# Fewer, larger transfers in a fused cross-attention and SwiGLU kernel: 220 transfers for 312

## The chip, the cores and the metric

The kernel runs on one core of a Trainium2 chip. The core has a matrix engine (TensorE, PE in the profile; the loading of its weights is listed apart as PEld), a vector engine (VectorE, DVE), an engine for activation functions and copies (ScalarE, ACT), a general one (GpSimd, POOL), and SyncE (SP), which issues transfers only. Transfers between the off-chip memory (DRAM) and the on-chip memory are issued from two queues here, SyncE's and ScalarE's, and are carried by 16 transfer engines. The metric is the time of one execution in microseconds on the device; the kernel before takes 755.71 us (median of 3 runs, 754.4 to 756.5).

## The reference

Eight batches with eight heads each; x has 512 tokens of 64 features per head, the state 32 rows per head. Cross attention runs both ways: tokens read the state, and state rows read the tokens. The results, 544 rows of 512 features per batch, then go through a normalisation and a gated feed-forward block.

```python
def _attn_ref(x, state):            # x (8, 8, 512, 64), state (8, 8, 32, 64)
    scores = scale * np.matmul(x, state.transpose(0, 1, 3, 2))
    ...
    xread = np.matmul(a, state)     # a = softmax of scores, over the state's rows
    scores2 = scale * np.matmul(state, x.transpose(0, 1, 3, 2))
    ...
    sread = np.matmul(a2, x)        # a2 = softmax of scores2, over the tokens
    return np.concatenate([xread, sread], axis=2)

def _moe_ref(x, w_gate, w_val, w_out, rms_g):   # x (4352, 512), w_gate (512, 1536)
    rms = np.sqrt(np.mean(x * x, axis=-1, keepdims=True) + 1e-06)
    xn = x / rms * rms_g
    g = xn @ w_gate
    silu = g * (1.0 / (1.0 + np.exp(-g)))
    return (silu * (xn @ w_val)) @ w_out
```

## The kernel before

The 512 tokens of a batch are worked on as one stage, batch after batch; the state rows of all batches together (256 rows) come last. For each batch TensorE multiplies the batch's state into the gate and value weights (`own_weights`, L703), runs the hidden layer as seven block products instead of eight (`hidden_seven`, L850), and the output projection as seven times seven quarter products (`project_twice`, L1153). The state rows go through `hidden_seven` and `project_seven` (L1016).

The order of all instructions is written out by hand. Each piece of work is a generator, a stream named by a letter, which yields after every step; strings of letters (ORDER, FIRST, PERIOD, LAST, STATES) say which stream takes its next step. Each engine runs its instructions, and issues its transfers, in exactly that order. While batch b is in its hidden layer and projection, the streams `a` (`tokens_read`) and `s` (`states_read`) prepare batch b + 1.

For batches 2 to 7, x has to be turned so that features lie on partitions. `scores` does that without TensorE: VectorE transposes blocks of 32 by 32 (L340) into `xB`, ScalarE's queue writes it to a scratch in DRAM (`x_d`, 1024 KB, L342) and reads it back with the blocks in another order (`xG`, four transfers of 256 KB, L347). A wait for the write stands in front of the first read, on ScalarE's queue. TensorE multiplies the result with the state (L357). In `states_read` the exponentials go the same way: transposed into `eB`, written to `e_d` (512 KB, L629), read back into `e2` (four transfers of 128 KB, L633), and multiplied with x (L644). Other instructions of ScalarE, such as the copies of the products out of TensorE's banks (L715, L897 to L904), stand in the same queue, between these issues.

In `project_twice`, ScalarE copies the partial products to a tile `kept` (L1163), VectorE adds more of them (L1193), GpSimd forms the four quarters from seven products in `combine` (L1179 to L1184), and `stores` sends two blocks of 128 rows by 256 columns through `store_tokens` (L1261) on SyncE's queue. `store_states` (L1268) writes the final state rows, one transfer per batch. `load_state` (L130) loads a batch's state with four transfers. Beside these SyncE fetches prepared weights (`w_m<-w_d`, L197, 1024 KB; `w<-t_d`, L1099, 576 KB).

## Time and profile before

| what | us |
| --- | --- |
| median of 3 runs (lowest, highest) | 755.71 (754.4, 756.5) |
| the profiled execution: time | 758.14 |
| the profiled execution: span | 756.4 |
| TensorE busy | 748.6 |
| VectorE, ScalarE, GpSimd busy | 580.0, 352.6, 296.3 |
| SyncE's transfers, share of the 16 engines' time | 46.4% |
| ScalarE's transfers, share of the 16 engines' time | 8.7% |
| granted TensorE clock, mean | 0.997 |

The profile comes from one execution. Its span runs from the first to the last instruction; the time of that execution also has what lies around the span. Each line of the profile names the line of the kernel, the engine and the operation, and the tiles as output<-input. A line of an engine with a q, such as ACTq or SPq, is the issue of a transfer by that engine's queue; the transfer itself lands later. In brackets stands how long an engine was idle before an instruction and what released it. Busy time of TensorE is modelled at its ends, so a busy TensorE is not one at its peak.

### The profile page before, as it was taken

To read this page: it belongs to the slowest core of one execution; us is meant where nothing else is said; L and a number is where in the kernel's file an instruction comes from. 1 tells how busy PE (TensorE), PEld (TensorE's weight loads), DVE (VectorE), ACT (ScalarE), POOL (GpSimd) and SP (SyncE) were. 2 spreads that over 40 slices of the span, in tenths; PEclk is the share of its full clock that TensorE was granted. 3 is DMA by queue.
4 is the path that set the end of the run, shared out by engine and by line. 5 is a ranking of instruction groups with operands and counts; after the bars stand their busy time and mean duration, and the time that the engine had idled before them with its cause. 6 is when DMAs were issued, how large, how long until landed. Compare 5 with 4: busy or idle time off the path is not lost.

```text
span 756.4 us, 14396 instructions
## 1 busy us (share of the span) xinstructions
PE 748.6 (99%) x5636; PEld 600.4 (79%) x5636; DVE 580.0 (77%) x982; ACT 352.6 (47%) x549; POOL 296.3 (39%) x387
## 2 busy tenths in 40 slices
PE   9999999999999999999999999999999999999998
PEld 7734344769978898879877997799788987899997
DVE  3989876569957996689848994799579965787962
ACT  4999892445245623644255425543456236411220
POOL 3100016961484227532465129312842275323600
PEclk9999999999999999999999999999999999999999
DMA  9787935861777186725673467517661865132411
GB/s 293 245 292 267 381 145 196 294 236 36 281 233 244 27 305 203 272 56 212 238 275 112 168 240 251 178 66 303 215 224 27 305 205 217 53 99 112 140 56 29
DMA packets 61891, 146.17 MB, mean 193 GB/s; under 512 B 15744, under 2 KB 32640, under 8 KB 54912
## 3 DMA queue, kind: packets, MB, share of 16 engines
q1 hardware_dynamic: 48704, 125.78, 46.4%
q10 hardware_dynamic: 13120, 19.47, 8.7%
q8 instruction: 45, 0.74, 0.4%
q14 instruction: 22, 0.18, 0.1%
HBM read 116.46 MB, written 28.77 MB: 192 GB/s over the span
## 4 chain that ended last, share of the span: by engine, by line
PE 94%; DVE 2%; POOL 2%; DMA 1%; issue 0%; ACT 0%; POOLq 0%
PE f L850 38%; PE f L1153 29%; PE f L953 6%; PE pv L746 6%; PE at L703 3%; PE pv L703 2%; PE f L1285 2%; PE f L1016 2%; DMA xG<-x_d 1%; PE at L357 1%; PE at L644 1%; PE at L450 1%; PE pv L517 0%; POOL w L1107 0%; PE at L308 0%
## 5 line engine op out<-in xcount | busy, mean ns | idle before, releaser
L850 PE MATMUL f<-aT_s,v 128*128 128x256 f32 x504 | 120.6, 384 | 0.0
L850 PEld LDWEIGHTS f<-aT_s,v 128*128 128x128 f32 x504 | 95.0, 191 | 24.4 <-issue 10.2
L1179 POOL TENSOR_TENSOR kept<-kept 128x256 f32<-128x256 f32 x28 | 23.1, 825 | 191.9 <-DVE kept L1193 190.7
L913 DVE TENSOR_TENSOR g<-g,f 128x512 f32<-128x512 f32 x84 | 57.4, 686 | 40.6 <-PE f L850 35.3
L1163 ACT COPY kept<-f 128x512 f32<-128x512 f32 (+1 forms) x56 | 29.7, 533 | 125.3 <-PE f L1153 83.4
L850 PE MATMUL f<-aT_t,vs 128*128 128x256 f32 x336 | 87.8, 385 | 0.2 <-POOL vs L730 0.2
L850 PEld LDWEIGHTS f<-aT_t,vs 128*128 128x128 f32 x336 | 63.2, 192 | 15.7 <-POOL vs L730 3.9
L1153 PE MATMUL f<-w,h 128*128 128x128 f32 x588 | 74.6, 276 | 0.0
L1153 PEld LDWEIGHTS f<-w,h 128*128 128x128 f32 x588 | 69.7, 192 | 4.9 <-issue 4.9
L904 ACT ACTIVATE hb<-g 128x1024 f32<-128x1024 f32 x42 | 44.4, 1058 | 54.9 <-DVE g L913 54.8
L730 POOL TENSOR_TENSOR vs<-v 128x256 f32<-128x256 f32 x42 | 31.7, 756 | 85.2 <-ACT v L715 85.2
L301 POOL TENSOR_TENSOR ri<-ss,mhalf 128x4 f32<-128x4 f32 (+1 forms) x9 | 12.5, 1385 | 98.9 <-DVE ss L382 67.6
L902 ACT COPY g<-f 128x512 f32<-128x512 f32 x42 | 24.6, 586 | 44.9 <-PE f L850 44.9
L953 PE MATMUL f<-wo,hb 128*128 128x512 f32 x96 | 44.9, 600 | 0.0
L746 PE MATMUL pv<-aT_s,v 128*128 128x512 f32 x96 | 44.1, 595 | 0.0
L850 PE MATMUL f<-aT_s,vs 128*128 128x256 f32 x168 | 43.6, 382 | 0.0
L926 DVE TENSOR_TENSOR hb<-hb,f 128x512 f32<-128x512 f32 (+1 forms) x48 | 31.1, 647 | 16.3 <-PE f L850 16.3
L850 PE MATMUL f<-aT_t,v 128*128 128x256 f32 x168 | 43.5, 381 | 0.0
L926 DVE TENSOR_TENSOR hb<-hb,c 128x512 f32<-128x512 f32 (+1 forms) x48 | 37.9, 789 | 6.6 <-ACT hb L904 5.9
L1153 PE MATMUL f<-wo,h 128*128 128x128 f32 x336 | 42.2, 275 | 0.0
L1153 PE MATMUL f<-wo,hb 128*128 128x128 f32 x336 | 42.1, 275 | 0.0
L913 DVE TENSOR_TENSOR c<-c,f 128x512 f32<-128x512 f32 (+1 forms) x48 | 31.3, 651 | 12.5 <-PE f L850 12.5
(225 smaller groups left out, 1678.2 us busy)
## 6 DMA issues: line engine op xcount, KB each, us to landing
w_m<-w_d SPq DMA_DIRECT2D x48, 1024.0 KB, 5.9
w<-t_d SPq DMA_DIRECT2D x49, 576.0 KB, 5.4
out_dram<-kept SPq DMA_DIRECT2D x56, 128.0 KB, 1.9
raw<-in_moe_w_val_dram SPq DMA_DIRECT2D x6, 1024.0 KB, 5.5
raw<-in_moe_w_out_dram SPq DMA_DIRECT2D x6, 1024.0 KB, 8.2
w_d<-w_m SPq DMA_DIRECT2D x6, 1024.0 KB, 4.9
x_b<-in_x_dram SPq DMA_DIRECT2D x6, 1024.0 KB, 7.4
x_d<-xB ACTq DMA_DIRECT2D x6, 1024.0 KB, 4.2
```

Of the source, the lines that this page charges most:

```text
L703: TE.matmul(out=pv[e][Ns * j:Ns * j + Ns, :], lhsT=stT_g[b][D * e:D * e + D, j, :], rhs=w[D * e:D * e + D, j].rearrange("p m k f -> p (m k ...
L730: GE.tensor_tensor(out=vs[:, 0], in0=a21, in1=a22, op=ALU.add)
L746: TE.matmul(out=to[0], lhsT=lhs(i, k), rhs=r, start=(i == 0), stop=(i == len(rhs) - 1))
L850: TE.matmul(out=ps[:, i, 0:half], lhsT=l[:, i, :], rhs=r, start=(start and i == 0 and k == 0), stop=(k == len(lhs) - 1), skip_group_check= ...
L902: SE.copy(gates(q)[1], q["x"][:, :, 0:half])
L904: SE.activation(out=hb[:, 2 * mp:2 * mp + 2, 0:n].rearrange("p m (c t) -> p m c t", c=2), in_=q["g"][:, :, :, 0:half], func=ACTF.Silu if s ...
L913: VE.tensor_tensor(out=to, in0=to, in1=q[ps][:, :, 0:half], op=ALU.add)
L926: VE.tensor_tensor(out=part, in0=part, in1=val, op=ALU.mult)
L953: TE.matmul(out=banks[r], lhsT=hb[:, m, P * r:P * r + P], rhs=wo[:, m, :], start=(m == 0), stop=(m == NM - 1))
L1153: TE.matmul(out=to[half][:, slot, :], lhsT=lhs[:, k, :], rhs=rhs[:, k, :], start=(fresh and n in (0, 4) and k == 0), stop=(k == QM - 1), s ...
L1163: SE.copy(k[:, 4 * i:4 * i + 4 - i], banks[name][i])
L1179: GE.tensor_tensor(out=k[:, 1:3], in0=k[:, 0:1].to_broadcast([P, 2, QD]), in1=k[:, 1:3], op=ALU.add)
```

## The change

Six kinds of transfer are merged; the number of transfers issued goes from 312 to 220. The scratch of x changes its layout so that a single transfer can write it (a partition's 2048 values as one run) and a single one can read it; the same holds for the exponentials. Where the reads were four steps of their stream, the one read is followed by empty steps (`yield from range(4)`), so that the strings of letters still fit. The token stores take 256 rows at once; for that the seven products lie in other slots of their banks and `combine` writes the quarters in the order in which they are stored. The final state rows of four batches go in one transfer, and the state rows of a batch come in two transfers instead of four.

```diff
     def load_state(b):
         rows[b] = two.tile([P, 2, D], F32, name="rows")
-        for j in range(4):
-            src = state[b, 2 * j:2 * j + 2].rearrange("e n d -> n e d")
-            nc.sync.dma_start(out=rows[b][Ns * j:Ns * j + Ns], in_=src)
+        for e in range(2):
+            nc.sync.dma_start(out=rows[b][:, e], in_=state[b, e::2])
...
-    x_d = [scratch.tile([4, 4, Ns, 4 * P], F32, name="x_d%d" % k) for k in range(2)]
-    e_d = [scratch.tile([4, Ns, 4, 8 * Ns], F32, name="e_d%d" % k) for k in range(2)]
+    x_d = [scratch.tile([Ns, 4, 4, 4 * P], F32, name="x_d%d" % k) for k in range(2)]
+    e_d = [scratch.tile([Ns, 4, 4, 8 * Ns], F32, name="e_d%d" % k) for k in range(2)]
...
-            nc.scalar.dma_start(out=x_d[b % 2].rearrange("q g f r -> (g f) q r"),
-                                in_=xB.rearrange("p q j c t -> p q (j c t)"))
+            nc.scalar.dma_start(out=x_d[b % 2].rearrange("f g q r -> g f (q r)"),
+                                in_=xB.rearrange("p q j c t -> p (q j c t)"))
             yield
             xT = one.tile([P, 4, 4, P], F32, name="xG", tag="xT")
-            for q in range(4):
-                nc.scalar.dma_start(
-                    out=xT[Ns * q:Ns * q + Ns].rearrange("f g j r -> f g (j r)"),
-                    in_=x_d[b % 2][q].rearrange("g f r -> f g r"))
-                yield
+            nc.scalar.dma_start(out=xT.rearrange("p g j r -> p g (j r)"),
+                                in_=x_d[b % 2].rearrange("f g q r -> q (f g) r"))
+            yield from range(4)
...
-            nc.scalar.dma_start(out=e_d[b % 2].rearrange("j t g f -> (j t) (g f)"),
+            nc.scalar.dma_start(out=e_d[b % 2].rearrange("t j g f -> j t (g f)"),
                                 in_=eB.rearrange("p g e c n -> p (g e c n)"))
             yield
-            for g in range(4):
-                nc.scalar.dma_start(out=e2T[Ns * g:Ns * g + Ns].rearrange("t j e c n -> t j (e c n)"),
-                                    in_=e_d[b % 2][:, :, g].rearrange("j t f -> t j f"))
-                yield
+            nc.scalar.dma_start(out=e2T.rearrange("p j e c n -> p j (e c n)"),
+                                in_=e_d[b % 2].rearrange("t j g f -> g (t j) f"))
+            yield from range(4)
...
-                        (0, 0, a11, b11), (0, 2, a12, b21), (0, 3, a22, 2), (0, 1, 1, 1),
-                        (1, 2, 0, 0), (1, 1, 2, b12), (1, 0, 3, b22))):
+                        (0, 1, a11, b11), (0, 0, a12, b21), (0, 2, a22, 2), (0, 3, 1, 1),
+                        (1, 0, 0, 0), (1, 1, 2, b12), (1, 2, 3, b22))):
...
+        def of_half(k, i):
+            return k[:, 1:4] if i else k[:, 4:8]
...
         def stores():
             for what in ("p1", "p5", "u2", "c21"):
-                for r in range(2):
-                    store(*ready[what][r])
-                    yield
+                store(*ready[what])
+                yield
+                yield

         def combine(what, i, j):
             k = kept[what]
-            ready[what] = []
-            GE.tensor_tensor(out=k[:, 1:3], in0=k[:, 0:1].to_broadcast([P, 2, QD]), in1=k[:, 1:3],
+            GE.tensor_tensor(out=k[:, 4:8:3], in0=k[:, 5:6].to_broadcast([P, 2, QD]), in1=k[:, 4:8:3],
                              op=ALU.add)
-            GE.tensor_tensor(out=k[:, 5:8:2], in0=k[:, 1:2].to_broadcast([P, 2, QD]),
-                             in1=k[:, 5:7], op=ALU.add)
-            GE.tensor_tensor(out=k[:, 1], in0=k[:, 5], in1=k[:, 6], op=ALU.add)
-            GE.tensor_tensor(out=k[:, 0:4:3], in0=k[:, 5:8:2], in1=k[:, 3:5], op=ALU.add)
-            for r in range(2):
-                at = 2 - 2 * r
-                ready[what].append((2 * i + r, HD * j, HD, k[:, at:at + 2].rearrange("p c f -> p (c f)")))
+            GE.tensor_tensor(out=k[:, 0:3:2], in0=k[:, 7:8].to_broadcast([P, 2, QD]),
+                             in1=k[:, 1:3], op=ALU.add)
+            GE.tensor_tensor(out=k[:, 7], in0=k[:, 2], in1=k[:, 1], op=ALU.add)
+            GE.tensor_tensor(out=k[:, 5:7], in0=k[:, 0:3:2], in1=k[:, 3:7:3], op=ALU.add)
+            ready[what] = 2 * i, HD * j, HD, k[:, 4:8].rearrange("p (r c) f -> p r (c f)", r=2)
...
     def store_tokens(b):
         def store(r, c0, n, ot):
-            rows_ = out[T * b:T * b + S, c0:c0 + n]
-            nc.sync.dma_start(out=rows_[P * r:P * r + P], in_=ot)
+            rows_ = out[T * b + P * r:T * b + S, c0:c0 + n].rearrange("(r p) f -> p r f", p=P)
+            if len(ot.shape) == 2:
+                nc.sync.dma_start(out=rows_[:, 0], in_=ot)
+            else:
+                nc.sync.dma_start(out=rows_[:, 0:2], in_=ot)
         return store

     def store_states(r, c0, n, ot, *more):
-        for j in range(4):
-            r0 = T * (4 * r + j) + S
-            queue = (nc.sync, *more)[j % (1 + len(more))]
-            queue.dma_start(out=out[r0:r0 + Ns, c0:c0 + n], in_=ot[Ns * j:Ns * j + Ns, :])
+        rows_ = out.rearrange("(b t) c -> b t c", t=T)[4 * r:4 * r + 4, S:T, c0:c0 + n]
+        (more or (nc.sync,))[0].dma_start(out=rows_, in_=ot)
```

Written as counts of steps from the outermost inward, the new transfers look so on their DRAM side, with 128 partitions on the other: x out 4 x 32 x 2048, x back 4 x 128 x 512, exponentials out 4 x 32 x 1024 and back 4 x 128 x 256, state rows in 4 x 32 x 64, state rows out 4 x 32 x 256, token stores 128 x 2 x 256. Before, each of these had 128 or 32 as its outermost count on both sides.

More of the change, by code (lines that the diff above doesn't have):

```diff
@@ L1162, in copies @@
                 for i in range(2):
-                    SE.copy(k[:, 4 * i:4 * i + 4 - i], banks[name][i])
+                    SE.copy(of_half(k, i), banks[name][i])
                     if what == "c21" and i:
@@ L1191, in add @@
             for n in range(2):
-                part = k[:, 4 * n:4 * n + 4 - n]
+                part = of_half(k, n)
                 VE.tensor_tensor(out=part, in0=part, in1=banks[name][n], op=ALU.add)
```

## The prediction, made before the run

> **What bounds the kernel now.** I read the page's first part and its chain, then what TensorE waited for, then the list of transfers, and last the order of time around the transfers that the change touches.
>
> The page: busy time of each engine, then the chain that ended last.
>
> ```profile
> span 756.4 us, 14396 instructions
> PE 748.6 (99%) x5636; PEld 600.4 (79%) x5636; DVE 580.0 (77%) x982; ACT 352.6 (47%) x549; POOL 296.3 (39%) x387
> ...
> PE 94%; DVE 2%; POOL 2%; DMA 1%; issue 0%; ACT 0%; POOLq 0%
> DMA packets 61891, 146.17 MB, mean 193 GB/s; under 512 B 15744, under 2 KB 32640, under 8 KB 54912
> ```
>
> TensorE is the bound: it is idle for under 8 us. So the change can win only what TensorE waits for, while any wait that it adds to TensorE costs in full. The next view, what TensorE waited for, shows how little there is to win.
>
> ```profile
> PE f L1285 <- POOL ident masks.py:199: 1.7, 1, 1.7
> PE at L357 <- DMA xG<-x_d: 1.7, 1, 1.7
> PE f L850 <- DVE hb L926: 0.5, 1, 0.5
> ```
>
> One wait of 1.7 us belongs to a transfer that the change touches: the read of x back from its scratch (xG<-x_d), in the first batch that takes that way. The order of time there, TensorE alone:
>
> ```profile
> 161.00 1.04 PE L357 MATMUL at<-xG,stT 64*32 64x512 f32 x2
> 163.70 1.24 PE L357 MATMUL at<-xG,stT 64*32 64x512 f32 x14 [1.65 <-DMA xG<-x_d]
> 164.87 2.07 PE L850 MATMUL f<-aT_s,v 128*128 128x256 f32 x4
> 166.74 1.62 PE L850 MATMUL f<-aT_t,vs 128*128 128x256 f32 x4
> 168.19 1.03 PE L850 MATMUL f<-aT_t,v 128*128 128x256 f32 x4
> ```
>
> A group of four such matmuls otherwise takes 1.03 us; after this pause the first takes 2.07 us and the second 1.62 us. The table by stretches gives the granted clock: 0.57 from 164 to 168 us, 1.00 before and after. Those 4 us at 0.57 cost 4 x 0.43 = 1.7 us, and with the start of the group about 2.0 us. So a pause of TensorE costs its length and some 2.0 us more.
>
> The transfers, with KB each and median us from issue to landing:
>
> ```profile
> out_dram<-kept SPq DMA_DIRECT2D x56, 128.0 KB, 1.9
> x_d<-xB ACTq DMA_DIRECT2D x6, 1024.0 KB, 4.2
> xG<-x_d ACTq DMA_DIRECT2D x24, 256.0 KB, 4.6
> e_d<-eB ACTq DMA_DIRECT2D x6, 512.0 KB, 3.1
> e<-e_d ACTq DMA_DIRECT2D x24, 128.0 KB, 3.3
> out_dram<-h SPq DMA_DIRECT2D x14, 32.0 KB, 1.6
> ```
>
> And an ordinary batch (the one that starts x at 236 us), ScalarE alone, whose queue issues these transfers between its copies; then the matmuls of L357 that read the result:
>
> ```profile
> 236.04 0.38 ACTq L342 DMA_DIRECT2D x_d<-xB  x1
> ...
> 242.42 1.28 ACTq L347 DMA_DIRECT2D xG<-x_d  x3
> 243.79 0.59 ACT L715 COPY v<-pv 128x512 f32<-128x512 f32 x1 [0.79 <-PE pv L703]
> 243.84 0.34 ACTq L347 DMA_DIRECT2D xG<-x_d  x1
> 249.56 1.09 PE L357 MATMUL at<-xG,stT 64*32 64x512 f32 x16
> ```
>
> From the write's issue to its reader are 13.5 us (249.56 less 236.04), and in it must fit a write, the wait of ScalarE for its landing, and a read. The same distance is 13.5 us in four of the five batches from the second on that go this way, 14.0 in the third of them. For the exponentials, the same two steps start at 283.85 (e_d<-eB) and their reader, L644, at 295.58: 11.7 us, equal in the five batches. These two distances are what the forecast is measured against.
>
> **The change, part by part.** Most edits have one answer. The state rows, 4 issues to 2 on SyncE's queue: one batch's four took 2.29 us of that queue (at 163.94), so about 1.1 us less each time; but SyncE is waited for by nobody on the chain, and their reader L319 comes later than the fetch by most of a batch. Nothing; without that cover a landing would cost up to 5.1 us, its median. Token stores, 56 of 128 KB to 28 of 256 KB: SyncE waits for POOL's last sum (L1184) as now, since both halves become ready with it. The larger one lands after 2.4 us (the 256 KB store of hs) instead of 1.9, and "kept" is taken again by later copies of ScalarE. Nothing, with 0.5 us per store at most if the buffer were short. The four sums on POOL in "combine" have the same four sizes (256, 256, 128, 256 elements), and the matmuls only change their slot in the bank: nothing, unless strided slots cost POOL more than the 0.73 us a sum that it takes for both strided and plain ones today. The steps kept as empty steps leave the order of all other instructions on TensorE, VectorE and ScalarE as it was; ScalarE loses 7 rows of issues.
>
> The state stores at the very end: two issues on ScalarE's queue after the last copy (753.34, 0.8 us for both, landing 1.6 us after issue) become one. That is 0.4 us less, if the one lands as fast.
>
> The x and exponential transfers are the matter, and what decides it is how many of the 16 transfer engines one transfer uses. Today's trace shows one spread only. Of the 15744 packets under 512 B, 8192 are the 256-byte rows of the eight x_b loads of batches 0 and 1 (8 x 256 KB), 2048 those of the rows (32 x 16 KB), and 512 the single values of rms_g (2 KB); 4992 are left, which is 16 x 312 transfers: each ends with 16 small packets, one per engine. And each of those 312 has 128 or 32 as its outermost count on both sides, which 16 divides. The new ones do not: the write of x goes to DRAM as 4 x 32 x 2048, the read takes it as 4 x 128 x 512; of the exponentials 4 x 32 x 1024 and 4 x 128 x 256; the state rows come as 4 x 32 x 64, the state stores go as 4 x 32 x 256. If the outermost steps are dealt out to the engines, those transfers reach 4 engines. No row of before has such a transfer, so I bound it: at the low end they use 16 engines as now and the change gains; at the high end they use 4, and moving the bytes takes four times as long. I take 4: the one pattern seen goes with outermost counts that 16 divides, and 4 outermost steps cannot be dealt to 16.
>
> [...]
>
> The prices, from the list above. 32 KB land after 1.6 us and 1024 KB after 4.2, so the bytes cost 2.7 us per MB on 16 engines and the fixed part is 1.5 us; on 4 engines, 10.7 us per MB. For reads the quickest of xG (256 KB, 3.1 us) leaves a fixed part of 2.4 us, and that of e (128 KB, 2.5 us) 2.2 us.
> - Write of x: 1.5 + 10.7 = 12.2 us (now 4.2). ScalarE stands at the read's issue until then, from 242.4 to 248.3 in the batch shown; queued behind it there are the copies of v (L715), the next gate (L904) and the copies of g and c that empty TensorE's banks, 1 to 9 us late.
> - Read of x: 2.4 + 10.7 = 13.1 us. Sum with 0.1 us for the wait's end: 25.4 us against the 13.5 there are. TensorE stops at L357 for 11.9 us; what ScalarE had late is made up inside that stop. With the restart of 2.0 us, 13.9 us a batch, and 69.5 us for five.
> - Write of e: 1.5 + 5.4 = 6.9 us; read of e: 2.2 + 5.4 = 7.6; with 0.1, 14.6 against 11.7: TensorE stops at L644 for 2.9 us. A restart after so short a stop I put at 1.5 us: between nothing (0.5 us of wait at L850, no slow group seen) and 2.0. 4.4 us a batch, 22 us for five.
> - The first batch that goes this way (x at 140.55, e at 202.97) has the load of the quarter weights beside it: its write of x now takes 6.5 us instead of 4.2, its write of e 4.8. With 2 to 4 us more per step, ScalarE stands from 147.7 to about 156, TensorE stops there and again at L357 until about 173, against 163.7 now: 10 us. For e, 9.7 us (212.63 less 202.97) against some 18: 8 us and the restart, 10 us.
> - The last state store: 128 KB on 4 engines, 1.5 + 1.3 = 2.8 us after one issue, against 1.6 after the second issue 0.4 us later: 0.8, say 1 us.
>
> Sum: 69.5 + 22 + 10 + 10 + 1 = 112.5 us. The profiled execution has a span of 756.4 us and a time of 758.1, 1.7 outside it; the span becomes 869, its time 870.6. The median of the runs shown, 755.7, lies 2.4 below the profiled one: 868 us.
>
> The ends within this case: low, the stop at L357 10.5 us with 1.0 for the restart, at L644 2.0 and none, the first batch 10, the end 0: 57.5 + 10 + 10 = 77.5, or 833 us. High, weight loads on the same four engines lengthen each x by 2 us and each e by 1.6, restarts 3 and 2, first batch 28, end 2: 85 + 32.5 + 28 + 2 = 147, or 903 us.
>
> **Rivals.**
> - *Faster: the merged transfers use all 16 engines.* Then one read of x, issued at 147.67 in the first batch instead of its last quarter at 155.59, lands after 2.4 + 2.7 = 5.1 us plus the load beside it, well before 161. The wait goes: 1.8 us and the 2.0 of restart. The end gains 0.4. 755.7 less 4 is 752 us, faster by 0.5%. For it: the bytes and packets are no more than now. Against: the counts of 4. The point from which it decides is the read's landing 13.5 us after the write's issue, which needs 9 engines or more.
> - *Only the writes are narrow.* 12.2 + 0.1 + 5.1 = 17.4 against 13.5: 3.9 and 2.0 a batch, 29.5 for five; e, 6.9 + 0.1 + 3.6 = 10.6, fits in 11.7. With 2 us for the first batch: 787 us. For it: a read's DRAM side with 128 inside could be dealt by that.
> - *Only the reads are narrow.* ScalarE reaches the issue at 242.4 anyway; 242.4 + 13.1 is 255.5 against 249.56: 5.9 and 2.0, 39.5 for five; e, 288.6 + 7.6 against 295.58: 0.6, 3 for five; first batch about 5: 803 us.
>
> **How the numbers follow.** Four engines on both ways: 0.78, 868 us, with 833 to 903 as its own range. One way only: 0.05 and 0.04. All 16: 0.13, 752 us. Within 0.3%, 2.3 us, nothing can be told from no change; of the 0.13, 0.02 falls there because the gain is only 4 us. So faster 0.11, same 0.02, slower 0.87. The range leaves out the fast case and the far ends of the first: 784 to 897 us.
>
> **What the profile after would show.** Right: x_d<-xB lands after about 12 us, xG<-x_d after about 13, e_d and e after about 7 each; TensorE's waits are led by L357 on xG (five stops of some 12 us, 70 us or so with the first) and L644 on e; groups at half pace behind each; under 512 B far fewer packets than 16 per transfer would make; the same instructions on TensorE. Wrong: landings of 4 to 5 us for 1024 KB, and no wait at L357. A size would be off if four engines move more each than they do among 16, or if the weight loads on SyncE's queue, which need the same four, come late and stop TensorE elsewhere.

## The result, and the profile after

The change makes the kernel slower: a median of 976.41 us (975.27 to 981.98, 6 runs) against 755.83 us (754.4 to 757.09, 6 runs) for the kernel before, measured beside it. The ratio is 1.2927 with an interval from 1.2893 to 1.2961. The profiled execution took 975.33 us with a span of 973.5 us, 217.1 us more than the span of before. The forecast was 868 us, from 784 to 897: the direction, the four engines and the two places came as predicted, but the time lies above the range; the loss is 220.6 us where 112.5 were forecast.

From the profile's page after the change, the engines, the packets, the two queues of transfers (packets, MB, share of 16 engines) and the chain that ended last:

```profile
span 973.5 us, 14251 instructions
PE 781.2 (80%) x5636; PEld 622.2 (64%) x5636; DVE 582.4 (60%) x982; ACT 352.7 (36%) x549; POOL 297.6 (31%) x387
...
DMA packets 57586, 146.15 MB, mean 150 GB/s; under 512 B 13744, under 2 KB 30640, under 8 KB 49840
...
q1 hardware_dynamic: 47532, 125.71, 36.7%
q10 hardware_dynamic: 9988, 19.53, 6.7%
...
PE 57%; DMA 31%; issue 7%; DVE 5%; ACT 1%; POOL 0%; ACTq 0%; DVEq 0%; POOLq 0%
```

TensorE has the same 5636 matmuls and is no longer the whole chain: transfers hold 31% of it. Of the 217.1 us, 184.5 are idle time of TensorE (192.3 us against 7.8), and 32.6 us are longer busy time for the same work, at a mean granted clock of 0.897. The bytes are the same 146 MB.

ScalarE's queue (q10) tells how many engines its transfers used, if each of these ends its part with one small packet, as the prediction read it. It moved 9988 packets, of which 9856 carry data (2 x 1024 for two loads of x_b, 6 x 128 and 6 x 512 for x out and back, the same again for the exponentials, 128 for one state store). The 132 that are left are the small packets at the end of a transfer which the prediction counted: 2 x 16 for the two loads and 25 x 4 for the 25 transfers with an outermost count of 4. Of these 25, the six reads of x, the six of the exponentials and the state store are merged; the twelve writes were single transfers before too, and only their layout changed. The same queue in the kernel before:

```profile
q10 hardware_dynamic: 13120, 19.47, 8.7%
```

There 12096 packets carry data, and 1024 are left, 16 for each of its 64 transfers. The two queues together agree: of the 13744 packets under 512 B after the change, 10752 carry data as before, and the other 2992 are 16 for each of 176 transfers and 4 for each of the 44 with an outermost count of 4. The busy share of the 16 engines agrees with that reading: between 262 and 304 us neither queue issues anything but x's write and read, and the share is 0.25 from 275 to 281 us (out) and 0.26 from 289 to 297 (back), near 4 of 16.

What TensorE waited for (us in total, times, longest), as it was read for the kernel before:

```profile
PE at L640 <- DMA e<-e_d: 80.7, 6, 14.5
PE at L354 <- DMA xG<-x_d: 69.3, 6, 12.4
PE f L846 <- ACT v L711: 24.1, 5, 4.8
PE f L846 <- ACT g L893: 11.2, 1, 11.2
PE f L1282 <- POOL ident masks.py:199: 1.7, 1, 1.7
```

The two readers that the prediction named stand at the head (L354 and L640 are L357 and L644 of before). The third and the fourth line are 35.3 us that TensorE waits for copies of ScalarE (L711, L893), which itself waits for the write of x to land. The prediction had such a stop in the first batch alone (L893); the five at L711 it had not.

The order of time in an ordinary batch, ScalarE's queue, ScalarE and TensorE; first x:

```profile
268.44 0.53 ACTq L341 DMA_DIRECT2D x_d<-xB  x1
...
282.97 0.53 ACTq L345 DMA_DIRECT2D xG<-x_d  x1
283.60 1.07 ACT L711 COPY v<-pv 128x512 f32<-128x512 f32 x2 [8.20 <-DMA x_d<-xB]
284.24 2.07 PE L846 MATMUL f<-aT_s,v 128*128 128x256 f32 x4 [4.79 <-ACT v L711]
...
299.63 1.96 PE L354 MATMUL at<-xG,stT 64*32 64x512 f32 x16 [10.43 <-DMA xG<-x_d]
301.52 2.07 PE L846 MATMUL f<-aT_t,vs 128*128 128x256 f32 x4
...
336.79 0.53 ACTq L626 DMA_DIRECT2D e_d<-eB  x1
...
349.20 0.54 ACTq L629 DMA_DIRECT2D e<-e_d  x1
...
363.07 1.94 PE L640 MATMUL at<-x_b,e 128*32 128x64 f32 x64 [14.49 <-DMA e<-e_d]
```

The write of x is issued at 268.44, and ScalarE stands at the read's issue until it has landed, 14.5 us later. Its copy of v is then late, and TensorE stops for 4.79 us. Then the read takes 16.7 us, and TensorE stops again, for 10.43. Each stop has a group at half pace behind it (2.07 us instead of 1.03; the granted clock from 298 to 304 us is 0.50). The exponentials take 12.4 us out and 13.9 back. The profile shows no landing times for these transfers, so a way out is read from the write's issue to the read's issue, and a way back from there to the reader.

The same two distances in all six batches (us), from the timelines of both kernels; the first batch has the load of the quarter weights beside it:

| from the write's issue to the reader | first | five others | five others, sum of the growth |
| --- | --- | --- | --- |
| x before | 20.5 | 13.5, 13.5, 14.0, 13.5, 13.5 | |
| x after | 45.6 (19.6 + 26.0) | 31.2, 31.2, 32.7, 33.2, 32.2 | 92.5 |
| exponentials before | 9.7 | 11.7 in each | |
| exponentials after | 19.1 (9.7 + 9.4) | 26.3, 25.8, 26.2, 26.2, 25.8 | 71.8 |

The first 20.5 us of x before end at the first two of the reader's 16 matmuls; the other 14 waited until 163.70, which makes 23.2. With the first batch (25.1 and 9.4) the growth is 198.8 of the 217.1 us. The other 18.3 us lie outside these distances. Slow groups behind the stop at each reader, twelve of them, would make 1.5 us each; that share is worked out from the remainder, not read group by group.

### The profile page after: what moved, and what is told of

The parts are those of the page before. It is cut to its first block, busy times and chain, and to the rows that moved or that the text cites. A ratio compares the mean times of both kernels' runs of the same rounds, so it can differ in the third digit from the quotient of the medians.

```text
span 973.5 us, 14251 instructions
## 1 busy us (share of the span) xinstructions
PE 781.2 (80%) x5636; PEld 622.2 (64%) x5636; DVE 582.4 (60%) x982; ACT 352.7 (36%) x549; POOL 297.6 (31%) x387
## 2 busy tenths in 40 slices
DMA packets 57586, 146.15 MB, mean 150 GB/s; under 512 B 13744, under 2 KB 30640, under 8 KB 49840
## 3 DMA queue, kind: packets, MB, share of 16 engines
q10 hardware_dynamic: 9988, 19.53, 6.7%
## 4 chain that ended last, share of the span: by engine, by line
PE 57%; DMA 31%; issue 7%; DVE 5%; ACT 1%; POOL 0%; ACTq 0%; DVEq 0%; POOLq 0%
PE f L846 20%; PE f L1149 16%; DMA xG<-x_d 12%; DMA x_d<-xB 9%; DMA e<-e_d 8%; PE f L949 4%; PE pv L742 4%; DMA e_d<-eB 2%; PE at L699 2%; PE f L1012 2%; PE f L1282 2%; PE at L640 1%; PE at L354 1%; PE pv L699 1%; DVE xB L339 1%
## 5 line engine op out<-in xcount | busy, mean ns | idle before, releaser
L846 PE MATMUL f<-aT_s,v 128*128 128x256 f32 x504 | 127.6, 398 | 24.1 <-ACT v L711 24.1
L1177 POOL TENSOR_TENSOR kept<-kept 128x256 f32<-128x256 f32 x28 | 23.1, 824 | 270.2 <-DVE kept L1189 269.1
L846 PE MATMUL f<-aT_t,vs 128*128 128x256 f32 x336 | 96.2, 414 | 11.2 <-ACT g L893 11.2
L846 PEld LDWEIGHTS f<-aT_t,vs 128*128 128x128 f32 x336 | 68.9, 209 | 32.2 <-issue 21.6
L640 PE MATMUL at<-x_b,e 128*32 128x64 f32 x512 | 13.8, 290 | 80.7 <-DMA e<-e_d 80.7
L726 POOL TENSOR_TENSOR vs<-v 128x256 f32<-128x256 f32 x42 | 31.2, 742 | 145.5 <-ACT v L711 145.5
L640 PEld LDWEIGHTS at<-x_b,e 128*32 128x32 f32 x512 | 12.2, 156 | 86.8 <-issue 86.8
L354 PE MATMUL at<-xG,stT 64*32 64x512 f32 x96 | 11.9, 1055 | 69.3 <-DMA xG<-x_d 69.3
L922 DVE TENSOR_TENSOR hb<-hb,c 128x512 f32<-128x512 f32 (+1 forms) x48 | 38.0, 792 | 32.7 <-ACT hb L900 31.9
L364 DVE STREAM_TRANSPOSE eS<-at 128x512 f32<-128x512 f32 x14 | 9.3, 698 | 74.3 <-PE at L354 74.3
L651 DVE TENSOR_SCALAR sr<-at,z 128x64 f32<-128x64 f32 x16 | 3.8, 278 | 80.4 <-PE at L640 80.4
L354 PEld LDWEIGHTS at<-xG,stT 64*32 64x32 f32 x96 | 1.7, 137 | 71.6 <-issue 71.6
L1179 POOL TENSOR_TENSOR kept<-kept 128x256 f32<-128x256 f32 x28 | 26.0, 929 | 69.7 <-ACT kept L1162 60.6
L711 ACT COPY v<-pv 128x512 f32<-128x512 f32 x42 | 23.0, 593 | 66.7 <-DMA x_d<-xB 41.1
```

Of the source, the lines that this page charges most:

```text
L640: TE.matmul(out=rp[Ns * j:Ns * j + Ns, e, :], lhsT=(e2T[:, j, e, c, :] if b > 1 else flat[:, e, c, Ns * j:Ns * j + Ns]), rhs=(xb[:, h, c, ...
L726: GE.tensor_tensor(out=vs[:, 0], in0=a21, in1=a22, op=ALU.add)
L846: TE.matmul(out=ps[:, i, 0:half], lhsT=l[:, i, :], rhs=r, start=(start and i == 0 and k == 0), stop=(k == len(lhs) - 1), skip_group_check= ...
L922: VE.tensor_tensor(out=part, in0=part, in1=val, op=ALU.mult)
L1179: GE.tensor_tensor(out=k[:, 0:3:2], in0=k[:, 7:8].to_broadcast([P, 2, QD]), in1=k[:, 1:3], op=ALU.add)
```

## The experiments

The theory to test was that of the prediction, four engines instead of sixteen, but with three questions open: which of the merges cost anything, what sets the price of a transfer on four engines, and whether the other queue's loads have a part in it.

**The merges one by one.** Three kernels. The first is the changed kernel with x and the exponentials taken back:

```diff
...
-            nc.scalar.dma_start(out=xT.rearrange("p g j r -> p g (j r)"),
-                                in_=x_d[b % 2].rearrange("f g q r -> q (f g) r"))
-            yield from range(4)
+            for q in range(4):
+                nc.scalar.dma_start(
+                    out=xT[Ns * q:Ns * q + Ns].rearrange("f g j r -> f g (j r)"),
+                    in_=x_d[b % 2][q].rearrange("g f r -> f g r"))
+                yield
...
```

> The change without its x and exponential transfers, which are as before; state rows, token stores, state stores and the quarter sums are as in the change. Theory A: the whole loss lies in x and the exponentials, so 755 to 756 us, same as before (0.4 us less at the end at best, 1 us more if four engines carry the last store). A rival, that a good part of the 220 us comes from the stores of 256 rows or from the sums in other slots, gives some tens of us more than before.

Measured: 756.81 us (12 runs) against 755.69 (17 runs), a ratio of 1.001 with an interval from 1.0001 to 1.0018. The merged token stores, state stores, state rows and the slots of the banks together are worth 0.2% at most, a loss if anything.

The other two are the kernel before with one of the two merges alone. x:

```diff
...
-            nc.scalar.dma_start(out=x_d[b % 2].rearrange("q g f r -> (g f) q r"),
-                                in_=xB.rearrange("p q j c t -> p q (j c t)"))
+            nc.scalar.dma_start(out=x_d[b % 2].rearrange("f g q r -> g f (q r)"),
+                                in_=xB.rearrange("p q j c t -> p (q j c t)"))
...
-            for q in range(4):
-                nc.scalar.dma_start(
-                    out=xT[Ns * q:Ns * q + Ns].rearrange("f g j r -> f g (j r)"),
-                    in_=x_d[b % 2][q].rearrange("g f r -> f g r"))
-                yield
+            nc.scalar.dma_start(out=xT.rearrange("p g j r -> p g (j r)"),
+                                in_=x_d[b % 2].rearrange("f g q r -> q (f g) r"))
+            yield from range(4)
```

> The kernel before with the x transfers of the change alone. From the changed kernel's trace, where the time from x's write to its reader grew by 17.7 us a batch and restarts by some 3.5: five batches 106 us, the first 21, so about 883 us. The forecast's own price for x was 80 us (836 us).

And the exponentials:

```diff
...
-            nc.scalar.dma_start(out=e_d[b % 2].rearrange("j t g f -> (j t) (g f)"),
+            nc.scalar.dma_start(out=e_d[b % 2].rearrange("t j g f -> j t (g f)"),
                                 in_=eB.rearrange("p g e c n -> p (g e c n)"))
...
-            for g in range(4):
-                nc.scalar.dma_start(out=e2T[Ns * g:Ns * g + Ns].rearrange("t j e c n -> t j (e c n)"),
-                                    in_=e_d[b % 2][:, :, g].rearrange("j t f -> t j f"))
-                yield
+            nc.scalar.dma_start(out=e2T.rearrange("p j e c n -> p j (e c n)"),
+                                in_=e_d[b % 2].rearrange("t j g f -> g (t j) f"))
+            yield from range(4)
```

> The kernel before with the exponentials' transfers of the change alone. From the changed kernel's trace, 14.6 us and 1.5 for the restart in five batches and some 11 in the first: 91 us, so about 847 us. The forecast's own price was 32 us (788 us).

Measured, in one run each: 881.93 us with x alone and 846.64 with the exponentials alone, beside 755.69. That is 126.2 and 91.0 us, together 217.2 of the 220.6. The two are the whole loss but for 3.4 us, and they add up: each stops TensorE at its own place (64.4 us in the first at the reader of x, 79.1 in the second at that of the exponentials).

**The transfers by themselves.** A kernel with nothing in it but a tile that goes out to scratch and comes back, one way after the other, with the size and the count of outermost steps on the DRAM side as its variables; on the way back the DRAM rows become longer as the count falls (1, 2 and 4 KB for 8, 4 and 2 engines at 1 MB), and with 16 engines the scratch is contiguous. In the program the last three pairs have two loads of 1 MB on SyncE's queue beside each way:

```diff
...
+    def by(k, n):
+        # outermost count k on the DRAM side, both ways
+        s = scratch.tile([P // k, k, k, n // k], F32, name="s%d_%d" % (k, n))
+        return (s.rearrange("f g q r -> g f (q r)"), s.rearrange("f g q r -> q (f g) r"), k)
...
+    for k, n, beside in ((16, 2048, 0), (8, 2048, 0), (4, 2048, 0), (2, 2048, 0), (16, 1024, 0),
+                         (4, 1024, 0), (4, 256, 0), (4, 2048, 1), (4, 1024, 1), (16, 2048, 1)):
```

> The kernel does none of the attention and none of the feed-forward block: it sends one tile out to a scratch and back, one transfer each way at a time, and only the outermost count of the DRAM side and the size differ; the last three pairs have two loads of 1 MB on the other queue beside each way. Theory A (the outermost count sets the number of engines, bytes then cost 2.7 us per MB on 16 of them in inverse proportion): 1 MB out takes 4.2 us for 128, 6.8 for 8, 12.2 for 4, 23 for 2; 1 MB back 5.1, 7.7, 13.1, 23.8; 512 KB out 2.9 for 128 and 6.9 for 4, back 3.6 and 7.6. With loads beside, a transfer on four engines waits for their share too (128 KB per engine, 5.4 us at most): 512 KB about 12 us a way, 1 MB 17 us, 1 MB on 16 engines 7 to 10. Theory B (one large transfer instead of four is what is slow, whatever its shape): the same times for 128, 8, 4 and 2. Theory C (the changed layout in DRAM, with rows of 8 KB apart by 32 KB, is what is slow): 8, 4 and 2 about alike, since all three have strided rows, and slower than 128.

Measured, from the timeline of that kernel: issue of the write and start of VectorE's step (L113) that waits for it, for 1 MB on 16, 8, 4 and 2 engines:

```profile
6.00 0.34 ACTq L109 DMA_DIRECT2D s<-a  x1
...
9.98 1.23 DVE L113 TENSOR_SCALAR a<-a 128x2048 f32<-128x2048 f32 x1 [0.35 <-DMA s<-a]
...
16.87 1.13 ACTq L109 DMA_DIRECT2D s<-a  x1
...
26.13 1.23 DVE L113 TENSOR_SCALAR a<-a 128x2048 f32<-128x2048 f32 x1 [9.30 <-DMA s<-a]
...
39.43 0.56 ACTq L109 DMA_DIRECT2D s<-a  x1
...
54.00 1.23 DVE L113 TENSOR_SCALAR a<-a 128x2048 f32<-128x2048 f32 x1 [14.60 <-DMA s<-a]
...
71.46 0.53 ACTq L109 DMA_DIRECT2D s<-a  x1
...
93.03 1.23 DVE L113 TENSOR_SCALAR a<-a 128x2048 f32<-128x2048 f32 x1 [21.61 <-DMA s<-a]
```

The loads did not always start where the program puts them. In the pair of 512 KB on four engines, one load was issued beside the way out and three beside the way back:

```profile
192.84 0.54 ACTq L109 DMA_DIRECT2D s<-a  x1
192.91 0.32 SPq L111 DMA_DIRECT2D w_x<-w_s  x1
...
204.54 0.32 SPq L112 DMA_DIRECT2D w_y<-w_s  x1
204.55 0.55 ACTq L117 DMA_DIRECT2D back<-s  x1
204.96 0.39 SPq L120 DMA_DIRECT2D w_x<-w_s  x1
...
209.75 0.32 SPq L121 DMA_DIRECT2D w_y<-w_s  x1
```

So the table gives the number of loads beside each way (the way back on 16 engines had a third, issued 0.8 us before its end):

| one way, us (out / back) | 16 engines | 8 | 4 | 2 |
| --- | --- | --- | --- | --- |
| 1 MB | 4.0 / 5.6 (beside another store from 8.39 us on) | 9.3 / 12.1 | 14.6 / 16.2 | 21.6 / 22.6 |
| 512 KB | 2.7 / 3.5 | | 10.1 / 8.2 | |
| 128 KB | | | 3.4 / 4.0 | |
| 1 MB, loads beside | 7.2 (one) / 8.1 (two) | | 19.0 / 22.2 (two each) | |
| 512 KB, loads beside | | | 10.9 (one) / 18.7 (three) | |

The small packets agree with the headings: this queue moved 5660 packets, 5504 with data, and the 156 that are left are twice the sum of the ten counts. The time goes with the number of engines, but not in inverse proportion. The prediction's line (1.5 us and 2.7 us per MB on 16 engines) gives 6.9, 12.2 and 22.9 us for 8, 4 and 2: eight and four take 2.4 us more than that, two take 1.3 less. And loads on the other queue lengthen a way on four engines: by 0.8 us (one load, 512 KB out), 4.4 and 6.0 (two, 1 MB) and 10.5 (three, 512 KB back). So no simple form of the theory holds: not four times, and not one engine with a fixed lower rate either, since two engines moved 24 KB/us each (1 MB in 21.6 us) and eight only 14.

**A possible reason why four and eight are worse than their share.** No run shows which engine takes which partitions. If 128 partitions are dealt out in order, which is assumed here, four engines start 32 partitions apart, eight 16 apart, two 64 apart. A kernel that sends half a tile, 64 partitions from partition 0 or from 32, with an outermost count of 2 or 4, changes only which partitions are sent:

```diff
...
-    for k, n, beside in ((16, 2048, 0), (8, 2048, 0), (4, 2048, 0), (2, 2048, 0), (16, 1024, 0),
-                         (4, 1024, 0), (4, 256, 0), (4, 2048, 1), (4, 1024, 1), (16, 2048, 1)):
+    for first, k in ((0, 2), (32, 2), (0, 4), (32, 4), (0, 2), (32, 2), (0, 4), (32, 4)):
...
-        nc.scalar.dma_start(out=to, in_=a[:, 0:n])
+        nc.scalar.dma_start(out=to, in_=a[first:first + 64])
```

> The kernel does none of the attention and none of the feed-forward block: it sends 64 partitions of a tile (512 KB) out to a scratch and back, one transfer each way at a time; the first partition is 0 or 32, the outermost count 2 or 4, each twice. The transfers alone had shown that 4 engines need some 3 us more, and 8 engines some 3 us more, than inverse proportion gives, while 2 engines did not. Theory D (two engines that start 32 partitions apart get in each other's way at first): from partition 0, counts 2 and 4 have such pairs, and each way takes 2 to 5 us longer than from partition 32, where the pairs are 32 to 63 against 64 to 95. From 32 a count of 2 takes 1.5 + 10.0 = 11.5 us out, a count of 4 takes 6.5; from 0 about 14 and 9.5. Theory E (few engines are slower for another reason, such as a later start of each, or the side of the DRAM): no difference between 0 and 32. [...]

Measured, the second pass of the four in that kernel's timeline, write's issue and VectorE's step that waits for it:

```profile
106.28 0.54 ACTq L100 DMA_DIRECT2D s<-a  x1
...
120.83 1.23 DVE L101 TENSOR_SCALAR a<-a 128x2048 f32<-128x2048 f32 x1 [14.58 <-DMA s<-a]
...
136.29 0.61 ACTq L100 DMA_DIRECT2D s<-a  x1
...
148.13 1.23 DVE L101 TENSOR_SCALAR a<-a 128x2048 f32<-128x2048 f32 x1 [11.87 <-DMA s<-a]
...
162.12 0.56 ACTq L100 DMA_DIRECT2D s<-a  x1
...
170.93 1.23 DVE L101 TENSOR_SCALAR a<-a 128x2048 f32<-128x2048 f32 x1 [8.84 <-DMA s<-a]
...
182.34 0.62 ACTq L100 DMA_DIRECT2D s<-a  x1
...
189.41 1.23 DVE L101 TENSOR_SCALAR a<-a 128x2048 f32<-128x2048 f32 x1 [7.11 <-DMA s<-a]
```

The same 512 KB with the same outermost count take 14.5 us from partition 0 and 11.8 from partition 32 (a count of 2), 8.8 and 7.1 (a count of 4). Dealt out in order, partitions 0 to 31 and 32 to 63 would be worked on side by side from partition 0; from 32, 32 to 63 and 64 to 95. The ways back agree: 14.2 and 12.7, 10.2 and 7.9. The first pass has the same order: 18.9 (with a store beside it), 11.9, 8.8 and 7.1 out, and 18.3, 12.9, 9.4 and 7.8 back.

So the half from partition 0 is the slower one in all four pairs, by 2.7 and 1.7 us out and by 1.5 and 2.3 back; theory D had 2 to 5. Why it is slower is not shown; with the order assumed, the engines start equally far apart in both kinds of half. Dealt out in that order, a transfer of 128 partitions on four engines would have partitions 0 to 31 and 32 to 63 side by side too, beside 64 to 127.

For 1 MB out this difference is as large as the excess over the price: a quarter of it, an engine's share, is 256 KB as in the half tile on two engines, and it took 14.6 us, against 14.5 in the half tile from partition 0 and 11.8 in that from 32, near the 12.2 of the prediction's price. It is not the whole account. The same comparison for the way back of 1 MB gives 16.2 against 14.2, and for 512 KB on four engines 10.1 against 8.8 out and 8.2 against 10.2 back. Nor is it shown why sixteen engines, which would hold both of these ranges too if the partitions were dealt out in the same order, take 4.0 us.

**Each way by itself.** The changed kernel with each write cut into four of 32 partitions, which have 32 as their outermost count, and the merged read kept:

```diff
-            nc.scalar.dma_start(out=x_d[b % 2].rearrange("f g q r -> g f (q r)"),
-                                in_=xB.rearrange("p q j c t -> p (q j c t)"))
+            for g in range(4):
+                nc.scalar.dma_start(out=x_d[b % 2][:, g].rearrange("f q r -> f (q r)"),
+                                    in_=xB[Ns * g:Ns * g + Ns].rearrange("p q j c t -> p (q j c t)"))
...
```

> The changed kernel, with its layout and its single reads, but each write of x and of the exponentials sent as four transfers, whose outermost count is 32 on both sides; the reads keep their outermost count of 4. Theory A: the writes land some 5 us after the first issue, the reads stay at 16.2 us (x) and 13.9 us (exponentials, with the weight loads beside). For x, 242.4 + 16.3 against 249.56 is 9.2 us and a restart of 2.5; for the exponentials, 289 + 13.9 against 295.58 is 7.3 and 1.5. Five batches 102 us, the first some 10: 868 us. If the writes were the whole cause: about 756 us. If the spread were not the cause: about 976 us as in the changed kernel.

And the other way round, the merged write kept and each read cut into four of 32 partitions, all four issued in one step:

```diff
-            nc.scalar.dma_start(out=xT.rearrange("p g j r -> p g (j r)"),
-                                in_=x_d[b % 2].rearrange("f g q r -> q (f g) r"))
+            for q in range(4):
+                nc.scalar.dma_start(out=xT[Ns * q:Ns * q + Ns].rearrange("f g j r -> f g (j r)"),
+                                    in_=x_d[b % 2][:, :, q])
             yield from range(4)
...
```

> The changed kernel, with its layout and its single writes (outermost count 4), but each read of x and of the exponentials sent as four transfers, whose outermost count is 32 on both sides, all four issued in the one step. Theory A: the write of x lands after 14.5 us, so the reads start at 250.6 instead of 242.4 and land at 256.9, 7.3 us after the time of their reader, and 2.5 for the restart; the write of the exponentials takes 12.4, its reads 4.7, 5.4 us late, and 1.5. Five batches 83 us, the first some 13: 852 us. If the reads were the whole cause: about 756 us.

Measured: 887.19 us with wide writes and narrow reads, 891.02 with narrow writes and wide reads (wide: an outermost count of 32, narrow: of 4). What TensorE waited for, in the first and then in the second:

```profile
PE at L355 <- DMA xG<-x_d: 55.1, 6, 11.0
PE at L642 <- DMA e<-e_d: 40.8, 6, 8.5
```

```profile
PE at L642 <- DMA e<-e_d: 59.8, 6, 11.7
PE f L848 <- ACT v L713: 34.3, 5, 7.1
PE f L848 <- ACT g L895: 13.2, 1, 13.2
```

Each way on four engines alone costs over 130 us (one run each), so neither is hidden by the other being short; both cost more than was expected. In the first kernel the read of x is issued 8.2 us after the write's first issue, with copies of ScalarE in between (6.4 before), and the way back of 14.8 to 18.0 us stops TensorE. In the second the stop at the read of x is gone (its distance is 14.5 + 7.5 to 8.7 us), and what is left for x is ScalarE, which stands until the write has landed: the five stops at L848 for v are those that the prediction had folded into the stop at the read. For the exponentials, the four wide reads are issued 12.3 to 13.6 us after the write, where that was 3.0 to 4.7 before, and their reader starts 9.1 to 11.2 us later. Why these four reads take so long, where the kernel before has a median of 3.3 us from issue to landing, is not shown. Both ways cut into four, in the new layout, was not run either.

**The loads beside.** The changed kernel with the prepared weights' loads left out from the third batch on:

```diff
-            nc.sync.dma_start(out=new_w(n), in_=w_d[n % (NM // 2)])
+            if 2 * (NM // 2) + 3 <= n < B * (NM // 2):
+                w_sb[n] = held_w[n % 3]
+            else:
+                nc.sync.dma_start(out=new_w(n), in_=w_d[n % (NM // 2)])
+                held_w[n % 3] = w_sb[n]
...
```

> The changed kernel, but from the third batch on the prepared weights are not fetched: three tiles of each kind that are already there are used again (so later batches use weights of other column blocks). That takes the two weight streams of SyncE's queue away from the four engines; all other instructions stay. Theory A2 (the exponentials' ways are so long in the kernel because the weight loads share the four engines): the way from the exponentials' write to their reader falls from 26.3 us to what the transfers alone took, 10.1 + 8.2 = 18.4, and x stays at 14.6 + 16.2 = 31; 7.9 us in five batches, about 936 us. Rival (the loads are no cause; the stores, or the exponentials' rows of 1 and 4 KB, are): the way stays at 26 us and the time at 976 us.

So these kernels use weights of the wrong columns in the later batches; only their time counts. The same edit in the kernel before:

> The same omission in the kernel before: from the third batch on no prepared weights are fetched. It shows what the omission alone is worth: TensorE waits for none of these loads in the kernel before, so 754 to 756 us.

Measured, in one run each: 955.02 us, 21.4 less than the changed kernel but more than the 936 expected, and 758.31 for the kernel before, beside 755.04. The waits of TensorE in the first:

```profile
PE at L359 <- DMA xG<-x_d: 68.5, 6, 13.1
PE at L645 <- DMA e<-e_d: 53.0, 6, 9.8
```

The wait for x stays (69.3 with the loads), that for the exponentials falls from 80.7 to 53.0 us. Their distance goes from a mean of 26.1 to 20.5 us, with 10.1 to 11.2 out (10.1 in the kernel with nothing but transfers) and 9.6 to 10.3 back (8.2). So the weight loads, without which the kernel before was no faster, lengthen each merged pair of the exponentials by some 5.5 us and x by little. The time falls by less than that wait, because TensorE is busy longer in the kernel without the loads (789.2 us against 781.2); why, is not shown. What is left of the loss is there without these loads.

**The gain of the faster rival.** It counted on the wait of 1.65 us at 163.70 in the first batch and the slow groups behind it: 4 us to win if x came back sooner. Two kernels bring it back sooner by other means, with the transfers as before. One issues the four reads in one step:

```diff
-                yield
+            yield from range(4)
```

> The kernel before, with its four reads of x issued in one step instead of four; nothing else is changed. It is the gain of the first rival without its merging: the first such batch's last quarter is issued with the others at about 149 us instead of at 155.59, lands before 157, and the wait of 1.8 us at 163.70 and the slow groups behind it (2.0 us) go. The rival's arithmetic gives 752 us, 0.5% faster. Against it: four issues in a row hold ScalarE for 1.4 us in front of its copies; if that costs as much as it gains, same as before, 755.7 us.

Measured: 757.76 us (11 runs), a ratio of 1.0026 (1.0014 to 1.0039). The wait at 163.70 is gone, but the four issues hold ScalarE, as its queue and TensorE show:

```profile
147.31 3.24 ACTq L347 DMA_DIRECT2D xG<-x_d  x4
...
151.38 1.10 PE L850 MATMUL f<-aT_t,vs 128*128 128x256 f32 x4 [1.37 <-ACT g L897]
```

TensorE waits 1.37 us for a copy behind them, and then at places where it did not wait before: 1.18 us for a step of VectorE, 0.83 for the exponentials (at 212.19) and 0.51 for another copy (at 221.58). From the list of its waits:

```profile
PE f L850 <- ACT g L897: 1.9, 2, 1.4
...
PE f L850 <- DVE c L913: 1.2, 1, 1.2
PE at L644 <- DMA e<-e_d: 0.8, 1, 0.8
```

The other kernel issues only the last read early, together with the third:

```diff
-                yield
+                if q != 2:
+                    yield
+            yield
```

> The kernel before, with the last of its four reads of x issued in the step of the third instead of its own; nothing else is changed. In the first such batch the issue moves from 155.59 to about 150 us, one issue at a time, so that ScalarE is not held for four issues in a row (which took 3.24 us with all four together). If the wait at 163.70 can be had: it lands before 157, L357 starts whole at 161, 1.8 us and the 2.0 of slow groups go, 752 us (ratio 0.995). If what is gained there comes back as another wait of TensorE, as with all four together: 755 to 758 us.

Measured: 755.78 us (12 runs) against 755.57 (17 runs), a ratio of 1.000 (0.999 to 1.001). Its profile shows the wait gone and a new one later:

```profile
159.99 1.09 PE L359 MATMUL at<-xG,stT 64*32 64x512 f32 x16
...
175.90 1.13 PE L852 MATMUL f<-aT_t,v 128*128 128x256 f32 x4 [1.19 <-DVE c L915]
```

The span is 753.7 us, 2.7 less than the profiled one of before; but that one was 2.4 us above the median of its kernel, and over the runs nothing can be told apart. The profile of the kernel with x and the exponentials taken back (756.91 us) has the same two features with the transfers of x as before: no wait at the read of x, and 1.18 us for the same step of VectorE later. So the wait at 163.70 comes and goes, and taking it away gains nothing that can be measured. The 4 us of the faster rival were not in it.

A single read with 32 or 128 as the outermost count on both sides, which would keep the merge and, going by the 16 small packets of each transfer with such counts, 16 engines, was not tried. Whether a merge in itself gains or loses is left open.

## Why the prediction was right about the direction and wrong about the size

- **Four engines: right.** All 44 transfers with an outermost count of 4 have four small packets each, and the two kernels with one merge alone (126.2 and 91.0 us) show that these transfers are the loss.
- **The other merges at nothing: right**, to 0.2% (ratio 1.001). That takes in the last state store, for which 1 us was added.
- **The places: right, the sizes at them not.** L357 and L644 of before lead the waits. That the wait at L357 comes to 69.3 us, where some 70 were forecast, is luck: the ways of x are 6.6 us a batch longer than priced, and 4.8 us of that stop fall on L711 instead. At L644 the stops are 14.0 to 14.5 us in the five batches, where 2.9 were forecast.
- **"On 4 engines, 10.7 us per MB": wrong**, and this is the first step that failed. The prices of 12.2 and 13.1 us for x and 6.9 and 7.6 for the exponentials took four engines for four times sixteen's time. By themselves they took 14.6 and 16.2, and 10.1 and 8.2. Per ordinary batch that is 5.5 us more for x and 3.8 for the exponentials, 46 us over five. Why, is not shown. One difference as large as the 2.4 us on x's way out was measured: a half tile with a count of 2 took 14.5 us from partition 0 and 11.8 from 32.
- **Weight loads only in the high end, at 1.6 us for the exponentials and 2 for x: wrong.** Taking the loads away in the changed kernel shortened the exponentials' distance by 27.6 us over the five batches, 5.5 in each, and that of x by 1.3 in all. The ways had to be priced with the loads beside them (1 MB back on four engines took 22.2 us beside two loads, 16.2 by itself).
- **"What ScalarE had late is made up inside that stop": wrong.** It is a stop of TensorE of its own, up to 4.8 us, ahead of the one at L354 in each of the five batches. Both lie inside the distance of some 32 us; the slow groups come twice.
- **The first batch, 10 and 10 us: too low for x.** The ways took 25.1 us longer for x and 9.4 for the exponentials, 34.5 in all with no restart in it. ScalarE stood until 159.02 where 156 was given, and the reader came at 184.97 where 173 was given. With loads beside, a way of 1 MB on four engines takes 19.0 and 22.2 us by itself; here it took 19.6 and 26.0.
- **The restarts: right for each, wrong in number.** The matmuls were busy 32.6 us longer in sum, and TensorE has 18 stops of this kind, three in each of six batches: 1.8 us for each, where 2.0 and 1.5 were put. But ten stops were counted in the five batches, where there are 15. That 18.3 us lie outside the distances, close to the 17.5 forecast, is chance: the slow groups behind the stops at L711 lie inside them.

The account of the miss, span against span: 217.1 less 112.5 is 104.6 us. The five x are 92.5 against 59.5 (33.0 more), the five exponentials 71.8 against 14.5 (57.3 more), the first batch 34.5 against 20 (14.5 more), the rest 18.3 against 18.5 (the near agreement of these last two is the chance just named). Of the 90.3 us in the five batches, 46 are the price of four engines by themselves and 29 the loads; about 15 are not pinned to a cause. The high end of 903 us was too near because it stacked the loads on a price that was itself too low: a stop at L644 of 2.9 us carried 22 us in the sum, and such a difference of two near numbers (14.6 less 11.7) becomes five times as large (26.1 less 11.7) when the first grows by four fifths.

The faster rival was wrong in its ground and in its arithmetic: the transfers don't use 16 engines, and the wait that it would have removed gives nothing when it is removed. The two rivals with one narrow way gave 787 us (the writes) and 803 (the reads); the kernels with one such way measured 891 and 887, with the same mis-sized price in them.

## What to carry to other kernels

Before merging transfers, write both sides of the new one as counts of steps from the outermost inward; here an outermost count of 4 meant 4 engines of 16, and 1 MB out took 14.6 us by itself instead of 4.0. Price such a transfer with a test of its own and with the loads that will run beside it, not by proportion from wide ones. And read the slack first: TensorE was idle for under 8 us, and by the prediction's own prices the two distances had 4 to 5 us to spare, so the merges could win at most a few us and lose two hundred.

## What was not expected of the hardware

Eight engines took 9.3 us for 1 MB out where sixteen took 4.0, and two took 21.6 where four took 14.6: the number of engines counts, and so does which partitions are sent (512 KB with an outermost count of 2 took 14.5 us from partition 0 and 11.8 from partition 32). The transfers of the other queue that use all engines hold up those on few: 1 MB back on four engines took 16.2 us by itself and 22.2 beside two loads of 1 MB, and 512 KB back 8.2 and, beside three, 18.7; 1 MB out on sixteen went from 4.0 to 7.2 beside one. Issues cost ScalarE time as well: the four issues of x's write in 32 partitions each took 2.72 us, where one of 128 partitions took 0.38 in the kernel before. And the stops of TensorE cost more than their length: around them its 5636 matmuls were busy 32.6 us longer in sum, at a mean granted clock of 0.897.
